# Residual sums in place, and four moves around the start of each attention layer

## The chip, the cores and the metric

The kernel runs on one core of one Trainium2 chip. The metric is device time in microseconds (us) of one execution, lower is better. The engines are named as in the profile: PE (matrix multiply; PEld is its weight load), DVE (vector), ACT (scalar, activations), POOL (GpSimd) and SP, whose queue issues nearly all DMAs. Each engine works through its own list of instructions in order and waits on semaphores for the others.

## The reference, cut to what matters

The input is one sequence of 2048 rows of 512 numbers. Four layers follow one another, spectral, attention, spectral, attention, and each adds its result to its input:

```python
x = x + A(layernorm(x)); x = x + B(layernorm(x)); x = x + A(layernorm(x)); x = x + B(layernorm(x))

A:  y = dft_seq_re @ (x @ dft_hid_re.T) - dft_seq_im @ (x @ dft_hid_im.T)

B:  q, k, v = x@wq, x@wk, x@wv            # 32 heads of 16, four segments of 512 rows
    for each segment s:
        a_dot = softmax(q_s k_s^T / 4 + causal mask) v_s
        a_mem = phi(q_s) M / (phi(q_s) z + 1e-6)         # phi(t) = t+1 if t>0 else exp(t)
        o_s   = sigmoid(beta) * a_mem + (1 - sigmoid(beta)) * a_dot
        M += phi(k_s)^T v_s;  z += sum of phi(k_s)
    return o @ wo
```

In the kernel the x that is added back is called the residual. In float32 each product is three matmuls over a high and a low part of both operands (`matmul3`, L106); `split` (L95) makes the two parts, the high one on ACT (L101) and the low one on DVE (L103).

## The kernel before, in words

The program is written as generators (a projection, a unit of softmax, a load with its split) that are placed into numbered slots by `place`; at the end the slots are run in order, and within a slot by a small order number. This gives the program order. PE keeps that order exactly. For the other engines and for the DMA queues a planner with a model of the times chooses the order, with the program order as priority; it may pull an instruction forward when the model shows its engine idle. Two kinds of instruction are pinned behind whatever stands just ahead of them on their engine in the program: the high part of a split on ACT, and the first statistics of a row, `bn_stats` (L139), on DVE. A tile with a tag shares a fixed number of buffers (`bufs`) with the others of that tag, and a new tile waits until a buffer is free.

A spectral layer ends with `hidden` for the first 1536 rows (products with the hidden DFT, 128 rows at a time into a PSUM tile `y`) and `hidden_last`, which works on four blocks of 128 rows at once, so that their four results come within a few matmuls of each other. Each result goes through `finish` (L164): DVE adds the residual rows `xr`, loaded with `load_rows` (L123), into a tile `xo`, and SP stores `xo` to DRAM (L167). `xo` has one buffer, so a sum waits until the store of the sum before has landed. All loaded rows (`xr`, the rows `xt` to be normalised, and raw weights `raw`) share the tag `xt` with four buffers of 2 KB per partition.

An attention layer has its own clock of slots; b is the slot at which its first unit starts. A unit is four heads of one segment; units follow every ten slots, eight in a segment of 80 slots, and two units make one head group g. For unit n at slot t = b + 10 n:

- `stack` loads its queries and keys (`stkq`, `stkk`) from DRAM, where the projection wrote them (`scrq`, `scrk`), at t - 21;
- `natural_max`, t - 17 to t - 7, makes the scores `nat` once to find each row's maximum: PE multiplies, DVE reduces (L605), then four small DVE operations (L621 to L628) write the maxima as three bf16 parts, `mparts`;
- `max_rows`, at t - 4, transposes `mparts` on PE into `mT`, ACT copies it to `mt` (L643), and a DMA on ACT's queue (L644) puts it into three extra rows of `stkq`;
- `softmax_values`, t to t + 12, makes the scores again, now with the maxima taken off (`sT`), the exponentials `pT`, and their product with the values (`pv_bank`).

What stands ahead of the first unit: `prep` normalises the rows of a segment, two blocks at a time: load, statistics, scaling to `xn` (L161), then PE transposes `xnT` and the split into `xT`. `proj` (PSUM tile `pqk`) makes queries and keys of one head group in 4 + 4 steps, `values` (`pvv`) makes the values in 16 steps. In the first segment head group 0 is projected from b - 34, the first eight steps of `values` stand at b - 26, head group 1 at b - 18, the second eight steps of `values` at b - 10. `hidden_last` of the spectral layer still runs from b - 26 to b - 12 beside them. The output weights `wo` are loaded and split by `load_split` at b - 14, b - 12, b - 10, b - 8, with the loads three slots sooner; the output projection that needs them first starts at b + 100. `prep` of the second segment has its transposes from b + 29 and b + 34 (t in the code), and its load, statistics and scaling 8, 5 and 3 slots ahead of that.

Of the kernel before, what the change touches and what calls it, by code (L numbers as in the profile page):

```python
# [10 lines left out]
F32 = mybir.dt.float32  # L11
# [3 lines left out]
ALU = mybir.AluOpType  # L15
# [3 lines left out]
P = 128  # L19
S, D, H = 2048, 512, 32  # L20
# [6 lines left out]
LT = L // P  # L27
# [34 lines left out]
def spectral_infini_kernel(  # L62
# [12 lines left out]
    nc = tc.nc  # L75
    V, A, G, T = nc.vector, nc.scalar, nc.gpsimd, nc.tensor

    consts = ctx.enter_context(tc.tile_pool(name="consts", bufs=1))
    sb = ctx.enter_context(tc.tile_pool(name="sb", bufs=1))
# [29 lines left out]
    def matmul3(ps, lhsT, rhs, first, last):  # L109
        T.matmul(ps, lhsT(0), rhs(0), start=first, stop=False)  # L110
        T.matmul(ps, lhsT(0), rhs(1), start=False, stop=False)
        T.matmul(ps, lhsT(1), rhs(0), start=False, stop=last)
# [4 lines left out]
    def bank(name, shape=(P, 512), dtype=F32):  # L117
        return psum.tile(list(shape), dtype, name=name, tag="bank", bufs=8)
# [2 lines left out]
        return sb.tile([P, 2, 512], dtype, name=name, tag=tag, bufs=bufs)  # L121

    def load_rows(src, name="xt"):  # L123
        t = sb.tile([P, 512], F32, name=name, tag="xt", bufs=4)
        nc.sync.dma_start(t, src)
        return t

# [7 lines left out]
    def row_stats(xts, mv):  # L135
        n = len(xts)
        for j, xt in enumerate(xts):
            st = sb.tile([P, 6], F32, name="st", bufs=2)
            pin(V.bn_stats(st, xt))  # L139
            V.bn_aggr(mv[:, j], st)  # L140
        ve = sb.tile([P, 2], F32, name="ve", bufs=3)[:, :n]
        V.tensor_scalar_add(ve, mv[:, :, 1], EPS)  # L142
        r = sb.tile([P, 2], F32, name="r", bufs=3)[:, :n]
        G.tensor_tensor(out=r, in0=ve, in1=half_neg[:, :n], op=ALU.pow)  # L144
        return ve, r

    def row_scale(rr, ve, r):
        t = sb.tile([P, 2], F32, name="rt", bufs=2)[:, : rr.shape[1]]
        V.tensor_tensor(out=t, in0=r, in1=r, op=ALU.mult)
        V.tensor_tensor(out=t, in0=t, in1=ve, op=ALU.mult)  # L150
        V.tensor_scalar(t, t, -0.5, 1.5, op0=ALU.mult, op1=ALU.add)
        V.tensor_mul(rr, r, t)
# [6 lines left out]
    def normal(xt, mv, rr):  # L159
        xn = sb.tile([P, D], F32, name="xn", bufs=2)  # L160
        V.tensor_scalar(xn, xt, mv[:, 0:1], rr, op0=ALU.subtract, op1=ALU.mult)  # L161
        return xn

    def finish(ps, xr, x_out, i, **where):  # L164
        xo = sb.tile([P, D], F32, name="xo", **(where or {"bufs": 1}))
        V.tensor_tensor(out=xo, in0=ps, in1=xr, op=ALU.add)  # L166
        nc.sync.dma_start(x_out[i], xo)  # L167
        return xo

    v_tiles = [consts.tile([P, H, VW], F32, name=f"vt{i}") for i in range(6)]  # L170
    v_count = [0]
# [7 lines left out]
    def place(order, gen, *at):  # L179
        for t in itertools.chain(*at):  # L180
            slots.setdefault(t, []).append((order, gen))

    def run_from(t, n, step=1):
        return range(t, t + n * step, step)
# [271 lines left out]
    def place_attention(x_in, x_out, t0, w_at, out_at):  # L456
# [3 lines left out]
        def prep(s, n):  # L460
            xt = [load_rows(x_in[s * LT + i]) for i in n]
            yield
            mv = sb.tile([P, 2, 2], F32, name="mv", bufs=2)
            ve, r = row_stats(xt, mv)
            yield
            rr = sb.tile([P, 2], F32, name="rr", bufs=2)
            row_scale(rr, ve, r)
            for j, i in enumerate(n):
                xn = normal(xt[j], mv[:, j], rr[:, j : j + 1])
                yield  # L470
                if i == 0:
                    xT[s] = sb.tile([P, 2, DT, 512], F32R, name="xT", bufs=1)
                pt = bank("xnT", (P, DT, P))
                for d in range(DT):
                    T.transpose(pt[:, d], xn[:, d * P : (d + 1) * P], ident)
                sl = slice(i * P, (i + 1) * P)
                split(xT[s][:, 0, :, sl], xT[s][:, 1, :, sl], pt)
                if j + 1 < len(n):
                    yield
            yield  # L480

        def values(s):
            vt[s] = {}
            for i in (0, 1, 3, 2):
                ps = bank("pvv")
                for d in range(DT):
                    matmul3(
                        ps,
                        lambda h: xT[s][:, h, d, i * P : (i + 1) * P],
                        lambda h: ws["v", d][:, h, :],  # L490
                        d == 0,
                        d == DT - 1,
                    )
                    if d + 1 < DT:
                        yield
                v = v_tiles[v_count[0] % len(v_tiles)]
                v_count[0] += 1
                A.activation(v[:, :, :DH], ps.rearrange("p (h d) -> p h d", d=DH), AF.Copy)
                vt[s][i] = v
                yield  # L500
# [390 lines left out]
        def outproj_split(s, i):  # L891
            n = (DT - 1) * P
            pt = bank("oT")
            for d in range(DT - 1):
                T.transpose(
                    pt[:, d * P : (d + 1) * P],
                    o_nat[s][i // 2][:, i % 2, d * P : (d + 1) * P],
                    ident,
                )
            t = pair("oh", "ut", 8)  # L900
            split(t[:, 0, :n], t[:, 1, :n], pt[:, :n])
            xr = load_rows(x_in[s * LT + i], "xr")
            yield
            ps = bank("po")
            for d in range(DT):
                src, c = (t, d) if d < DT - 1 else (oh[s, "last"], i)
                matmul3(
                    ps,
                    lambda h: src[:, h, c * P : (c + 1) * P],
                    lambda h: ws["o", d][:, h, :],  # L910
                    d == 0,
                    d == DT - 1,
                )
                yield
            finish(ps, xr, x_out, s * LT + i, tag="wd", bufs=8)
            yield

        def alloc_pv():
# [17 lines left out]
        def light(t, n=SU):  # L936
            return [k for k in range(t, t + n) if (k - t0) % SU not in (2, 4)]
# [5 lines left out]
        def post(t):  # L943
            return [t + 1, t + 2, t + 3]

        for k in range(4 * DT):
            n, d = "qkvo"[k // DT], k % DT
# [3 lines left out]
        for n in range(NSEG * USEG):  # L951
            t = t0 + SU * n
# [5 lines left out]
        for s in range(NSEG):  # L958
            b = t0 + SS * s
            for j in range(2):  # L960
                t = b - (43, 51, 60, 60)[s] + 5 * j
                place(2, prep(s, (2 * j, 2 * j + 1)), [t - 8, t - 5, t - 3, t, t, t + 2])
            place(2, values(s), *([light(b - 20), light(b)] if s else [run_from(b - 26, 8), light(b - 10)]))
            place(2, alloc_out(s), [b - 13])
            o = b + SS
            if s < NSEG - 1:
                free = light(o + 20) + light(o + 40) if s < NSEG - 2 else run_from(o + 20, DT * LT, 3)
            else:
                free = [out_at(k) for k in range(4 * LT)]
            if s == NSEG - 1 and x_out is out_tiles:  # L970
                for i in range(LT):
                    place(2, outproj_split(s, i), [o - 12 + i], range(o - 7 + 3 * i, o - 7 + 3 * i + 3), [o + 5 + 1, o + 7])
                place(1.5, transpose_last(s), [o + 5])
            else:
                for i in range(LT):
                    at = free[DT * i : DT * (i + 1)]
                    place(2, transpose_out(s, i), [at[0] - 4 - i % 2])
                    place(2, outproj(s, i), at)
            for g in range(NG):
                t = b + SG * g  # L980
                late = [] if s or g > 1 else [b + 3 + 2 * g]
                at = {
                    (0, 0): run_from(b - 34, 8),
                    (0, 1): run_from(b - 18, 8),
                    (0, 2): among(b, b + 13, 8),
                    (0, 3): among(b + 13, b + 29, 8),
                    (1, 0): among(b - 40, b - 29, 8),
                    (1, 1): among(b - 29, b - 17, 8),
                }.get((s, g), light(t - 50))
                place(2, proj(s, g, "q"), at[:4], post(at[3]))  # L990
                place(2, proj(s, g, "k"), at[4:], post(at[7]), late)
                if s > 0:
                    place(2, mem_read(s, g), [t - 12, t - 8])
                if s < NSEG - 1:
                    place(2, mem_update(s, g), [t + 6, t + 9] if g else [t + 16, t + 19])
# [11 lines left out]
    b2 = a2 + TC * 7 * HALF + LEAD  # L1007

    def w_at(b):
        return lambda k: b - 52 + 2 * k if k < 12 else b - 14 + 2 * (k - 12)  # L1010

    place_spectral(
        x_tiles, mids[0], a1, b1 - LEAD,
# [90 lines left out]
```

## Time and profile before

| | us |
|---|---|
| median of three runs (lowest, highest) | 1871.7 (1870.88, 1874.08) |
| profiled execution: time / span from first to last instruction | 1868.32 / 1866.6 |
| PE busy in the span | 1781.6 |
| first attention layer: first `mT` / first `pv_bank` of unit 0 | 479.66 / 497.55 |
| second attention layer: first `mT` | 1388.26 |

The times of the profile are microseconds from the first instruction. A row of the timeline gives start, duration, engine, line, operation, output tile <- input tiles, shapes, how many alike were merged, and in square brackets how long the engine had stood idle just before and what released it. PE's rows run into each other because a matmul's start overlaps the end of the one before. A row of the windows gives for a stretch A:B its length and the busy time and instruction count of PE, PEld, DVE, ACT and POOL, then the mean granted PE clock (1.00 is full speed), the DMA engines' busy share and GB/s. SPq and ACTq are the DMA issues of these engines.

### The profile page before, as it was taken

What the parts mean: (1) busy time and instruction counts of PE and PEld (TensorE: products, weight loads), DVE (VectorE), ACT (ScalarE), POOL (GpSimd) and SP (SyncE); (2) the same over time, 40 slices, a digit from 0 to 9 for tenths busy, and PEclk for the clock granted to TensorE, in tenths of its full rate; (3) what the DMA queues carried; (4) which work ended last, traced back from release to release, by engine and by line L of the source; (5) the groups of instructions that cost most, each with busy time, mean ns of one, the idle gap of its engine ahead of it and who ended that gap; (6) DMA issues with size and microseconds to landing.
All of it is one profiled execution on the core that took longest, in us unless ns stands there. A gap on an engine that the chain in (4) does not pass through costs nothing. (4 is left out here: it accounts for less than half of the span.)

```text
span 1866.6 us, 32022 instructions
## 1 busy us (share of the span) xinstructions
PE 1781.6 (95%) x10336; PEld 1291.0 (69%) x10336; DVE 1315.2 (70%) x4073; ACT 1056.1 (57%) x2292; POOL 526.1 (28%) x831
## 2 busy tenths in 40 slices
PE   7999999999889999999899999999988999999998
PEld 6788888888556666665468888778865566666555
DVE  7854544663787887877967686768557778787684
ACT  3222221432678787778864455444427877777785
POOL 4400000003345354445542000000124444444442
PEclk9999999999999999999999999999998999999999
DMA  6766556453534443435357687654544334344331
GB/s 214 225 217 214 189 181 210 161 170 127 177 125 134 131 134 104 147 119 181 106 170 231 196 259 215 180 170 141 172 144 142 121 113 150 120 132 136 121 122 51
DMA packets 165656, 296.50 MB, mean 159 GB/s; under 512 B 17776, under 2 KB 66928, under 8 KB 165488
## 3 DMA queue, kind: packets, MB, share of 16 engines
q1 hardware_dynamic: 162224, 293.68, 49.9%
q8 instruction: 81, 1.33, 0.3%
q10 hardware_dynamic: 3264, 0.79, 0.2%
q14 instruction: 87, 0.71, 0.1%
HBM read 192.95 MB, written 100.66 MB: 157 GB/s over the span
## 5 line engine op out<-in xcount | busy, mean ns | idle before, releaser
L605 DVE CUSTOM_DVE_ANT_0 junk<-nat,mask 128x512 bf16<-128x512 f32 (+3 forms) x1024 | 496.3, 485 | 196.6 <-PE nat L87 162.2
L671 ACT ACTIVATE pT<-sT 128x512 f32<-128x512 f32 x640 | 371.5, 599 | 13.5 <-ACT sT L670 1.7
L674 POOL TENSOR_SCALAR_AFFINE_SELECT pT<-pT 128x256 f32<-128x256 f32 (+1 forms) x448 | 198.6, 457 | 451.8 <-ACT pT L671 388.1
L87 PE MATMUL u<-chi,xa 128*128 128x512 f32 x1024 | 317.3, 391 | 7.3 <-DVE xa L99 7.3
L87 PE MATMUL sT<-stkq,stkk 99*128 99x256 bf16 (+3 forms) x1024 | 249.1, 306 | 10.1 <-DMA stkq<-mt 4.6
L87 PE MATMUL nat<-stkk,stkq 96*128 96x512 bf16 (+3 forms) x1024 | 247.0, 303 | 7.1 <-DVE mx L605 2.7
L670 ACT ACTIVATE sT<-sT 128x256 f32<-128x256 f32 (+1 forms) x640 | 207.3, 335 | 53.0 <-PE sT L87 48.3
L87 PEld LDWEIGHTS u<-chi,xa 128*128 128x128 f32 x1024 | 193.5, 189 | 47.2 <-ACT chi L101 7.3
L144 POOL TENSOR_TENSOR r<-ve,half_neg 128x2 f32<-128x2 f32 (+1 forms) x33 | 22.7, 688 | 665.2 <-DVE ve L142 660.1
L87 PE MATMUL u<-clo,xa 128*128 128x512 f32 x512 | 201.5, 394 | 2.4 <-DVE clo L103 2.0
L87 PE MATMUL y<-wdt,us 128*128 128x512 f32 x768 | 181.9, 390 | 0.0
L87 PEld LDWEIGHTS <-stkk 99*128 99x128 bf16 x1024 | 82.2, 99 | 136.7 <-issue 122.9
L87 PEld LDWEIGHTS y<-wdt,us 128*128 128x128 f32 x768 | 143.6, 188 | 29.7
L87 PE MATMUL pv_bank<-pT,vt 128*17 128x512 f32 (+3 forms) x2048 | 151.2, 435 | 0.0
L87 PEld LDWEIGHTS <-stkq 96*128 96x128 bf16 x1024 | 94.6, 99 | 62.4 <-issue 22.8
L87 PE MATMUL pvv<-wv,xT 128*128 128x512 f32 x384 | 129.8, 451 | 3.7 <-DVE mx L605 3.7
L87 PE MATMUL pqk<-xT,wq 128*128 128x512 f32 x384 | 130.3, 448 | 0.0
L87 PE MATMUL po<-wo,oh 128*128 128x512 f32 x384 | 122.3, 433 | 4.2 <-DVE mx L605 2.2
L87 PE MATMUL pqk<-xT,wk 128*128 128x512 f32 x384 | 124.7, 433 | 0.0
L87 PEld LDWEIGHTS u<-clo,xa 128*128 128x128 f32 x512 | 96.6, 189 | 26.6 <-DVE clo L103 6.7
L87 PEld LDWEIGHTS pv_bank<-pT,vt 128*17 128x17 f32 x2048 | 53.6, 97 | 85.9 <-issue 82.7
L101 ACT ACTIVATE chi<-cring 128x512 fp32r<-128x512 f32 x112 | 70.6, 630 | 69.3 <-DVE clo L103 35.0
(138 smaller groups left out, 3038.3 us busy)
## 6 DMA issues: line engine op xcount, KB each, us to landing
sum<-sring SPq DMA_DIRECT2D x32, 1024.0 KB
cring<-sum SPq DMA_DIRECT2D x128, 256.0 KB
stkq<-scrq SPq DMA_DIRECT2D x64, 384.0 KB
stkk<-scrk SPq DMA_DIRECT2D x64, 384.0 KB
cring<-in_ct SPq DMA_DIRECT2D x96, 256.0 KB
sring<-in_ct SPq DMA_DIRECT2D x32, 512.0 KB
xt<-mid SPq DMA_DIRECT2D x64, 256.0 KB
craw<-in_ct SPq DMA_DIRECT2D x30, 512.0 KB
```

What stands on the lines that cost most here:

```text
L87: return tc.keep_in_program_order(op(*args, **kwargs))
L101: pin(A.activation(hi, src, AF.Copy, scale=scale))
L144: G.tensor_tensor(out=r, in0=ve, in1=half_neg[:, :n], op=ALU.pow)
L605: V.tensor_tensor_reduce(junk[:, :n], src, mask[:, 512 - n :], 1.0, 3e38, ALU.add, ALU.min, dst,)
L670: A.activation(blocks, blocks, AF.Relu)
L671: A.activation(dst, ps, AF.Exp, scale=-SCALE)
L674: G.affine_select(blocks, blocks, pattern=[[0, n] for n in blocks.shape[1:-1]] + [[1, P]], compare_op=ALU.is_ge, fill=0.0, base=0, channel ...
```

## The change

It has five parts, in both attention layers alike, and the arithmetic is the same.

1. `finish` adds into the loaded residual tile itself and stores from there. The tile `xo` is gone, in the last output projection too, where it had the tag `wd`; the row tag `xt` gets a fifth buffer. The memory is the same. A row buffer is now held until its store has landed.
2. The output weights are loaded and split at b + 20, b + 25, b + 30, b + 35.
3. Head group 1 of the first segment is projected from b - 26.
4. The first eight steps of the first segment's `values` move to b - 18.
5. `prep` of the second segment has its load, statistics and scaling 18, 14 and 10 slots ahead of the transposes. The transposes stay.

```diff
     def load_rows(src, name="xt"):
-        t = sb.tile([P, 512], F32, name=name, tag="xt", bufs=4)
+        t = sb.tile([P, 512], F32, name=name, tag="xt", bufs=5)
...
-    def finish(ps, xr, x_out, i, **where):
-        xo = sb.tile([P, D], F32, name="xo", **(where or {"bufs": 1}))
-        V.tensor_tensor(out=xo, in0=ps, in1=xr, op=ALU.add)
-        nc.sync.dma_start(x_out[i], xo)
-        return xo
+    def finish(ps, xr, x_out, i):
+        V.tensor_tensor(out=xr, in0=ps, in1=xr, op=ALU.add)
+        nc.sync.dma_start(x_out[i], xr)
...
-            finish(ps, xr, x_out, s * LT + i, tag="wd", bufs=8)
+            finish(ps, xr, x_out, s * LT + i)
...
-                place(2, prep(s, (2 * j, 2 * j + 1)), [t - 8, t - 5, t - 3, t, t, t + 2])
-            place(2, values(s), *([light(b - 20), light(b)] if s else [run_from(b - 26, 8), light(b - 10)]))
+                first = (18, 14, 10) if s == 1 else (8, 5, 3)
+                place(2, prep(s, (2 * j, 2 * j + 1)), [*(t - d for d in first), t, t, t + 2])
+            place(2, values(s), *([light(b - 20), light(b)] if s else [run_from(b - 18, 8), light(b - 10)]))
...
-                    (0, 1): run_from(b - 18, 8),
+                    (0, 1): run_from(b - 26, 8),
...
-        return lambda k: b - 52 + 2 * k if k < 12 else b - 14 + 2 * (k - 12)
+        return lambda k: b - 52 + 2 * k if k < 12 else b + 20 + 5 * (k - 12)
```

## Prediction

> **What bounds the kernel now.** I read the page's busy times first, then PE's waits over the whole span, then the timeline of PE around the longest of them, and last what DVE and the DMA queue did there.
>
> ```profile
> PE 1781.6 (95%) x10336; PEld 1291.0 (69%) x10336; DVE 1315.2 (70%) x4073; ACT 1056.1 (57%) x2292; POOL 526.1 (28%) x831
> ...
> PE xnT L87 <- DVE xn L161: 18.2, 6, 4.8
> PE mT L87 <- DVE mparts L628: 13.1, 6, 5.5
> ...
> PE nat L87 <- DMA stkk<-scrk: 2.3, 1, 2.3
> ```
>
> PE sets the time: it is busy for 95% of the span, and its order is fixed. So only its idle time (85 us) and its clock can change much. The two largest waits are for the rows of a later segment (xnT) and for the first unit's maxima (mT). PE's timeline shows where they fall:
>
> ```profile
> 479.66 0.33 PE L87 MATMUL mT<-ident_b,mparts 128*80 128x128 bf16 x1 [4.97 <-DVE mparts L628]
> 479.75 1.63 PE L87 MATMUL pvv<-wv,xT 128*128 128x512 f32 x3
> 486.18 0.39 PE L87 MATMUL sT<-stkq,stkk 99*128 99x256 bf16 x2
> 486.44 1.04 PE L87 MATMUL pqk<-xT,wq 128*128 128x512 f32 x3
> 497.55 2.35 PE L87 MATMUL pv_bank<-pT,vt 128*17 128x512 f32 x32
> 511.14 2.35 PE L87 MATMUL pv_bank<-pT,vt 128*17 128x512 f32 x32
> 526.30 1.09 PE L87 MATMUL xnT<-ident,xn 128*128 128x128 f32 x4 [4.80 <-DVE xn L161]
> 529.88 2.52 PE L87 MATMUL pv_bank<-pT,vt 128*17 128x512 f32 x32
> ...
> 1388.26 0.33 PE L87 MATMUL mT<-ident_b,mparts 128*80 128x128 bf16 x1 [5.48 <-DVE mparts L628]
> 1394.47 0.39 PE L87 MATMUL sT<-stkq,stkk 99*128 99x256 bf16 x2
> 1411.30 0.58 PE L87 MATMUL nat<-stkk,stkq 96*128 96x512 bf16 x1 [2.30 <-DMA stkk<-scrk]
> 1437.32 1.09 PE L87 MATMUL xnT<-ident,xn 128*128 128x128 f32 x4 [4.79 <-DVE xn L161]
> ```
>
> The same two waits stand in both attention layers, and a third (nat, 2.30) in the second one only. After each the same matmuls are slow (three of pvv take 1.63, three of pqk later 1.04). The windows around them give the clock:
>
> ```profile
> 474.69:486.18 11.49, 6.52 (x20) 4.11 (x19) 8.96 (x35) 2.02 (x4) 0.79 (x1) 0.70 0.90 277
> 521.00:541.00 20.00, 13.94 (x99) 8.21 (x98) 18.86 (x68) 13.67 (x33) 7.14 (x13) 0.83 0.48 152
> 474.69:541.00 66.31, 54.07 (x356) 33.43 (x356) 54.27 (x217) 46.74 (x112) 25.89 (x43) 0.90 0.50 157
> 541.00:581.00 40.00, 39.23 (x288) 24.48 (x286) 31.02 (x125) 33.90 (x82) 21.01 (x32) 1.00 0.41 130
> 1382.78:1394.47 11.69, 6.21 (x19) 3.90 (x19) 9.81 (x36) 2.53 (x5) 1.22 (x1) 0.71 0.89 289
> 1410.00:1420.00 10.00, 8.70 (x44) 5.94 (x45) 5.70 (x27) 6.08 (x15) 3.25 (x7) 0.83 0.24 83
> 625.00:635.00 10.00, 7.84 (x69) 5.11 (x70) 9.79 (x31) 5.92 (x13) 6.17 (x9) 1.00 0.69 215
> ```
>
> A wait is paid twice: a mean of 0.70 over 11.49 us is 6.9 us at half speed. The row to remember for later is the second: DVE is busy 18.86 of 20 us.
>
> **Why the first maxima are late.** The DVE rows ahead of the first mT, and the DMA queue's:
>
> ```profile
> 471.76 0.69 DVE L166 TENSOR_TENSOR xo<-y,xr 128x512 f32<-128x512 f32 x1 [0.40 <-DMA mid<-xo]
> 475.20 0.08 DVE L605 DVE_READ_ACCUMULATOR2_ANT mx<- 128x1 f32 x1
> 476.56 0.69 DVE L166 TENSOR_TENSOR xo<-y,xr 128x512 f32<-128x512 f32 x1 [1.28 <-DMA mid<-xo]
> 477.16 0.17 DVE L621 SCALAR_TENSOR_TENSOR mparts<-mx 128x16 bf16<-128x16 f32 x1
> 477.86 0.69 DVE L103 TENSOR_TENSOR wo<-raw,wo 128x512 fp32r<-128x512 f32 x1
> 478.84 0.68 DVE L103 TENSOR_TENSOR wo<-raw,wo 128x512 fp32r<-128x512 f32 x1
> 479.44 0.17 DVE L628 SCALAR_TENSOR_TENSOR mparts<-mrem,mparts 128x16 bf16<-128x16 f32 x1
> ...
> 422.07 0.38 SPq L125 DMA_DIRECT2D raw<-in_wo  x1
> 468.07 0.35 SPq L125 DMA_DIRECT2D xr<-in_x  x1
> 468.47 0.42 SPq L167 DMA_DIRECT2D mid<-xo  x1
> 1390.65 0.32 SPq L576 DMA_DIRECT2D stkk<-scrk  x1
> ```
>
> Unit 0's last maximum is read at 475.20, and mparts is ready only at 479.6. In between DVE, in its own order, stood 1.28 for a store so that it could write the single xo, made that sum (0.60 to the next start), and put two splits of wo (0.60 from 478.84 to 479.44) between the four small operations. Before 475.20 it had lost 0.40 to another store, and two more wo splits and a phi of head group 1 there. A raw wo loaded at 422.07 also held one of four row buffers until its split, so that the last residual came only at 468.07.
>
> **The change part by part, against the profiled execution** (1868.32 us, span 1866.6; the median of the runs is 3.4 above it, and I carry the gain over to the median).
>
> A. Sums in place, wo away from here, head group 1 ahead of the values. The swap itself moves as many matmuls one way as the other, both from tiles that are ready, and the values are first used by pv_bank at 497.55; I cost it at nothing, covered by these 30 us; if that cover went, PE would wait for one ACT copy, some 0.6. DVE's remaining work up to the maxima (four sums, and reductions that follow PE) fits ahead of the moment at which PE reaches mT (479.66 - 4.97 = 474.69). So that wait goes. What is late next is the way from mT over ACT and the DMA into stkq, which the undisturbed end of this layer shows:
>
> ```profile
> 929.29 0.25 PE L87 MATMUL mT<-ident_b,mparts 128*80 128x128 bf16 x1 [1.14 <-DVE mparts L628]
> 933.90 0.59 PE L87 MATMUL sT<-stkq,stkk 99*128 99x256 bf16 x2 [3.71 <-DMA stkq<-mt]
> ```
>
> It takes 933.90 - 929.29 = 4.6. PE's work between mT and sT is 6.52 at about half speed, some 3.5 at full. The stage then lasts 4.6, of which 1.1 is a new wait at sT, instead of 11.49 and 11.69: 6.9 + 7.1 = 14.0 gained. Bounds: with the maxima still 2 late in each layer 10; with no new wait 16.
>
> B. Head group 1 written eight slots sooner. In the second layer unit 2's keys are loaded at 1390.65, because their projection ends late, and PE waits 2.30. Eight slots of about 1.36 us (ten take 511.14 - 497.55 = 13.6) are 11 us: the wait goes. The clock row 1410 to 1420 (0.83) is 3.4 us at half speed, about 2.9 of it after the wait: 1.45. Together 3.75; the first layer has no such wait. [...]
>
> C. Rows of the second segment ten slots sooner. The loads were early anyway; the statistics and scaling were not:
>
> ```profile
> 477.64 0.43 SPq L125 DMA_DIRECT2D xt<-mid  x1
> ...
> 518.24 0.68 DVE L139 BATCH_NORM_STATS2 st<-xt 128x6 f32<-128x512 f32 x1
> 525.61 1.00 DVE L161 TENSOR_SCALAR xn<-xt,mv,rr 128x512 f32<-128x512 f32 x2
> ...
> 630.12 0.63 PE L87 MATMUL xnT<-ident,xn 128*128 128x128 f32 x4 [2.16 <-DVE xn L161]
> ```
>
> Scaling moves by seven slots, 9.5 us; xn ended at 526.6 and would end near 517, while PE arrives at 526.30 - 4.80 = 521.5. The wait goes, 4.80 and 4.79; the clock row 521 to 541 (0.83) is 6.8 us at half speed, some 3.8 of it after the wait until pv_bank is normal again at about 530: 1.9 in each layer. Together 13.4. The waits of 2.16 in later segments stay.
>
> D. DVE pays. From 474.69 to 541 it is busy 54.27 of 66.31. Two sums and two wo splits move ahead of this stretch or out of it (4 x 0.60), leaving 51.9; the four wo splits come back at b + 20 to b + 35, 54.3 in all. After A and C the stretch would be 66.31 - 6.9 - 6.7 = 52.7. DVE's best share there is 18.86 of 20, 94%; at that it needs 55.2 without the splits and 57.8 with them, 2.5 or 5.1 too much. The planner can let splits slip into 541 to 581, where DVE has 9 us free; I take the middle, 3.8 in each layer, 7.6 lost. Bounds: 0, and all of C (6.7 in each layer). ACT gets the four high parts too, about 0.6 each, and is busy 46.74 of the 66: it follows.
>
> E. The fifth row buffer and the longer hold. A store issued at 468.47 released the sum at 471.76: 3.3 us longer for each buffer. Four residuals of hidden_last need four buffers and the fifth takes a row of segment two; residual loads stand far ahead of their sums (all but the one that wo held up). I take 0; a loss bound is one exposed store in each of the four layers, 13, and a gain 2. SP's queue gets fewer blocked issues before the first unit, and four loads more among the stacks, 256 KB each, beside DMA engines that are busy half the time.
>
> Sum: 14.0 + 3.75 + 13.4 - 7.6 = 23.6. 1868.3 becomes 1844.7, and the median 1871.7 becomes 1848.
>
> **The rivals.**
>
> *DVE takes back most of C.* For it: the share of 94% without the splits. One set of maxima in each layer then comes late by a few us, as at 929.29, and the next sT waits 3.71 and runs slow for about 1.9: 2 x 5.6 = 11 less gain, 1859. Against it: reductions have priority, and DVE has free time from 486 to 521.
>
> *Slower.* The same shortage, but lasting: wo splits and statistics stand in front of the maxima of units 2 to 5 in both layers. A late set costs what A is worth, about 7 to 8. It decides from the fourth of the eight units on (4 x 7 = 28 against 23.6); with all eight, 1848 + 56 = 1904, with five 1883. Against it: even in 521 to 541 the mT there waited little, and the splits can be done any time until b + 100.
>
> *The change doesn't do what it says.* DVE's order is the planner's: it may still put the sums between the last reduction and mparts. Then A saves only the stands for a store and the wo splits, 0.40 + 1.28 + 1.2 in each layer with the clock still dropping: about 6 instead of 14, 1856.
>
> *More gain.* DVE's shortage costs nothing (D is 0) and the new wait at sT doesn't show: 1848 - 7.6 - 2.2 = 1838.
>
> **How the numbers follow.** Forecast (1842 to 1855) 0.54; most of C taken back 0.20; planner keeps the sums 0.08; more gain 0.08; slower 0.10. The 8 in 10 range reaches from the gain case to somewhat above the first rival, 1838 to 1864. The measurement tells about 0.2%, 3.7 us, from no change. All cases but the slower one are faster; 0.03 from their edge may end within 0.2%: faster 0.87, same 0.03, slower 0.10.
>
> **What the profile after would show.** A: mT of unit 0 with an idle time below 1 in both layers, no wait for a store ahead of L166, the clock at 1.00 there, and a wait of about 1 at the first sT for stkq<-mt. B: no nat wait for stkk. C: bn_stats right after the pv_bank of unit 0, xnT of the second segment without a wait. D: wo splits among the maxima of units 2 to 4, DVE above 90% there, and small waits of PE on L605 or mparts. E: no PE wait for y or po on xr. The prediction is wrong if the time lost at unit 0 turns up whole in units 2 to 5, or if PE waits at the spectral layers' rows.

## The result, and the profile after

| | before | after |
|---|---|---|
| median (lowest to highest), five runs each on one chip, us | 1870.88 (1868.13 to 1874.08) | 1852.11 (1848.91 to 1853.03) |
| ratio after / before, 95% interval | | 0.9896 (0.9883 to 0.991) |
| profiled execution: time / span, us | 1868.32 / 1866.6 | 1848.91 / 1847.2 |

The kernel is 1.0% faster: 18.8 us by the medians, 19.4 by the profiled executions. The forecast was 1848 (1838 to 1864). The total hides that two of the five steps, A and B, came out for another reason than the one given; the experiments below show it.

The page of the kernel after, busy times, and PE's waits over the whole span (us in total, times, longest):

```profile
PE 1775.4 (96%) x10336; PEld 1284.1 (70%) x10336; DVE 1315.7 (71%) x4073; ACT 1054.6 (57%) x2292; POOL 526.3 (28%) x831
...
PE xnT L87 <- DVE xn L161: 9.8, 5, 2.2
...
PE mT L87 <- DVE mparts L626: 6.8, 9, 1.4
PE sT L87 <- DMA stkq<-mt: 6.5, 5, 3.8
```

The work is the same (10336 matmuls, DVE 0.5 us apart). The waits for rows fell from 18.2 to 9.8 and those for maxima from 13.1 to 6.8; the waits for `stkq<-mt` grew from 4.6 to 6.5. PE's busy time fell by 6.2, and the mean granted clock of the profiled execution rose from 0.989 to 0.997. PE's timeline after, at the places shown of before:

```profile
475.05 0.25 PE L87 MATMUL mT<-ident_b,mparts 128*80 128x128 bf16 x1 [0.53 <-DVE mparts L626]
478.71 0.40 PE L87 MATMUL sT<-stkq,stkk 99*128 99x256 bf16 x2
490.30 2.35 PE L87 MATMUL pv_bank<-pT,vt 128*17 128x512 f32 x32
504.13 2.35 PE L87 MATMUL pv_bank<-pT,vt 128*17 128x512 f32 x32
515.92 0.60 PE L87 MATMUL xnT<-ident,xn 128*128 128x128 f32 x4
518.09 2.35 PE L87 MATMUL pv_bank<-pT,vt 128*17 128x512 f32 x32
526.51 0.25 PE L87 MATMUL mT<-ident_b,mparts 128*80 128x128 bf16 x1 [1.42 <-DVE mparts L626]
532.12 2.35 PE L87 MATMUL pv_bank<-pT,vt 128*17 128x512 f32 x32
...
620.28 1.09 PE L87 MATMUL xnT<-ident,xn 128*128 128x128 f32 x4 [2.14 <-DVE xn L161]
921.05 0.25 PE L87 MATMUL mT<-ident_b,mparts 128*80 128x128 bf16 x1 [1.13 <-DVE mparts L626]
925.71 0.58 PE L87 MATMUL sT<-stkq,stkk 99*128 99x256 bf16 x2 [3.77 <-DMA stkq<-mt]
1296.27 0.66 PE L87 MATMUL xnT<-ident,xn 128*128 128x128 f32 x4 [1.20 <-DVE xn L161]
1376.51 0.25 PE L87 MATMUL mT<-ident_b,mparts 128*80 128x128 bf16 x1 [0.52 <-DVE mparts L626]
1521.98 0.63 PE L87 MATMUL xnT<-ident,xn 128*128 128x128 f32 x4 [2.16 <-DVE xn L161]
```

DVE's timeline has the four sums in one piece, with no wait for a store:

```profile
467.18 2.73 DVE L165 TENSOR_TENSOR xr<-y,xr 128x512 f32<-128x512 f32 x4 [0.57 <-PE y L87]
```

The 4.97 and 5.48 at the first mT are 0.53 and 0.52; the 4.80 at the second segment's rows is gone (515.92 has no bracket), and so is the nat wait of 2.30. New are the 1.42 at 526.51 (and the same at 1428.21) and the 1.20 at 1296.27. The windows give the clock:

```profile
474.52:478.71 4.19, 3.67 (x19) 2.33 (x19) 3.73 (x18) 0.67 (x2) 0.00 (x0) 1.00 0.27 67
518.09:532.12 14.03, 11.02 (x85) 5.79 (x84) 13.21 (x49) 12.48 (x31) 4.15 (x8) 1.00 0.66 209
610.00:630.00 20.00, 17.34 (x119) 11.71 (x117) 18.73 (x62) 14.35 (x35) 10.37 (x16) 0.91 0.48 150
1515.00:1535.00 20.00, 16.84 (x124) 11.52 (x123) 19.54 (x69) 14.69 (x35) 9.39 (x16) 1.00 0.54 172
915.00:935.00 20.00, 15.11 (x108) 8.88 (x101) 15.50 (x49) 14.63 (x34) 11.22 (x17) 0.83 0.41 132
```

The stage from the first mT to the first sT is the first row: 4.19 us at 1.00, where before it was 11.49 at 0.70. Half clock is what the windows show inside a slow stretch: 0.50 from 480 to 482 before, 0.50 from 621 to 623 after. The second row is where DVE is full now: 13.21 of 14.03 busy, and PE stands for 3.0 of it.

Where the 19.4 us came from can be read unit by unit, from the start of each unit's `pv_bank` before and after (497.55 - 490.30 = 7.25 for unit 0, and so on). Each row after the first is what that one unit adds to the gain; units that add or lose less than 0.8 are left out, but for unit 1. Unit 32 is the first of the second attention layer.

| unit | gained, us |
|---|---|
| unit 0 | 7.25 |
| unit 1 | -0.24 |
| unit 2 | 4.78 |
| unit 3 | -1.94 |
| unit 9 (the clock after the wait at 620.28) | -1.59 |
| unit 32 | 5.98 |
| unit 33 | 2.24 |
| unit 34 | 4.77 |
| unit 35 | -1.78 |

### The profile page after: what moved, and what is told of

It is laid out like the page before. It is cut to its first block, busy times and chain, and to the rows that moved or that the text cites. A ratio compares the mean times of both kernels' runs of the same rounds, so it can differ in the third digit from the quotient of the medians.

```text
span 1847.2 us, 31988 instructions
## 1 busy us (share of the span) xinstructions
PE 1775.4 (96%) x10336; PEld 1284.1 (70%) x10336; DVE 1315.7 (71%) x4073; ACT 1054.6 (57%) x2292; POOL 526.3 (28%) x831
```

## The experiments

The first five kernels each undo or shift one part of the change; the other six do one part alone, extend it, or test what was left. A ratio is against the kernel before on the same chip, with its 95% interval. "Lost" and "gained" at a unit are read like the table above, against the kernel after unless another is named. A stand is time in which an engine has an instruction next in its order but must wait for its input or its buffer.

**The separate sum tile put back** (four row buffers as before, the rest as after).

```diff
-        t = sb.tile([P, 512], F32, name=name, tag="xt", bufs=5)
+        t = sb.tile([P, 512], F32, name=name, tag="xt", bufs=4)
...
-    def finish(ps, xr, x_out, i):
-        V.tensor_tensor(out=xr, in0=ps, in1=xr, op=ALU.add)
-        nc.sync.dma_start(x_out[i], xr)
+    def finish(ps, xr, x_out, i, **where):
+        xo = sb.tile([P, D], F32, name="xo", **(where or {"bufs": 1}))
+        V.tensor_tensor(out=xo, in0=ps, in1=xr, op=ALU.add)
+        nc.sync.dma_start(x_out[i], xo)
+        return xo
...
-            finish(ps, xr, x_out, s * LT + i)
+            finish(ps, xr, x_out, s * LT + i, tag="wd", bufs=8)
```

> The changed kernel with the separate sum tile xo (one buffer) and four row buffers again; the other four parts stay. Theory: the store that each sum waits for is a part of A of its own. Four sums 3.3 us apart end some 10 us after the first, past the moment at which PE reaches the first mT, so a wait of 2 to 4 and half speed come back there: 6 to 14 us of the 19.4 are lost, ratio to before 0.993 to 0.997. Rival: the wo splits alone made the maxima late; then the first mT waits under 1 us and the ratio is that of the changed kernel, 0.988 to 0.991.

Measured: 1849.41, ratio 0.9893 (0.9867 to 0.9918), the same as the kernel after, as the rival has it. Its timeline of PE at the first mT:

```profile
476.20 0.25 PE L87 MATMUL mT<-ident_b,mparts 128*80 128x128 bf16 x1 [1.20 <-DVE mparts L628]
```

Its timeline of DVE at the same place:

```profile
470.75 0.69 DVE L166 TENSOR_TENSOR xo<-y,xr 128x512 f32<-128x512 f32 x1
...
473.77 0.69 DVE L166 TENSOR_TENSOR xo<-y,xr 128x512 f32<-128x512 f32 x1
...
476.57 0.69 DVE L166 TENSOR_TENSOR xo<-y,xr 128x512 f32<-128x512 f32 x1
```

The sums are still 3 us apart; with one `xo`, each has to follow the store of the one before. But none of these three has an idle time ahead of it: reductions fill the gaps. mT waits 1.20 instead of 0.53, and unit 0 starts 1.78 later. In the first layer 1.61 of that comes back at unit 9: the kernel after has its clock drop there, at 620.28, and its slowest `xnT` takes 0.45, while no `xnT` of this execution takes over 0.33. In the second layer unit 32 is level: the first mT waits 1.01 instead of 0.52, but the wait at 1296 isn't there. The stands for a store were not what made the maxima late.

**The output weights put back to their slots.**

```diff
-        return lambda k: b - 52 + 2 * k if k < 12 else b + 20 + 5 * (k - 12)
+        return lambda k: b - 52 + 2 * k if k < 12 else b - 14 + 2 * (k - 12)
```

> The changed kernel with the output weights at b - 14 to b - 8 again. Theory: two to four splits of 0.6 us and the row buffer held by a raw weight are the other part of A: the first mT waits 2 to 4 us in each layer, partly with half speed, 6 to 14 us lost, but units 2 to 4 get 2 x 2.4 us of DVE time back, so 2 to 10 lost in all, ratio 0.991 to 0.995. Rival: the stores alone made the maxima late; then the first mT waits under 1 us, and D is smaller: ratio 0.987 to 0.989, better than the changed kernel.

Measured: 1858.45, ratio 0.9941 (0.9923 to 0.9959). Its timeline of PE at the first mT:

```profile
478.80 0.33 PE L87 MATMUL mT<-ident_b,mparts 128*80 128x128 bf16 x1 [4.26 <-DVE mparts L626]
```

Its timeline of DVE ahead of that, the rows of the weights:

```profile
468.49 0.68 DVE L103 TENSOR_TENSOR wo<-raw,wo 128x512 fp32r<-128x512 f32 x1
...
472.97 0.69 DVE L103 TENSOR_TENSOR wo<-raw,wo 128x512 fp32r<-128x512 f32 x1 [0.96 <-ACT wo L101]
...
475.35 0.69 DVE L103 TENSOR_TENSOR wo<-raw,wo 128x512 fp32r<-128x512 f32 x1 [0.88 <-ACT wo L101]
...
477.59 0.69 DVE L103 TENSOR_TENSOR wo<-raw,wo 128x512 fp32r<-128x512 f32 x1
```

And its timeline of ACT, where two high parts wait for the load:

```profile
472.31 0.63 ACT L101 ACTIVATE wo<-raw 128x512 fp32r<-128x512 f32 x1 [1.53 <-DMA raw<-in_wo]
...
474.69 0.63 ACT L101 ACTIVATE wo<-raw 128x512 fp32r<-128x512 f32 x1 [1.75 <-DMA raw<-in_wo]
```

This is the old wait, with every other part of the change in place: 4.26 here and 4.52 in the second layer. Four splits of 0.60 are 2.4, and the two stands are 0.96 + 0.88, together 4.2; the mT starts 3.75 later than in the kernel after (478.80 against 475.05), so DVE could make up a little. The stands are a chain of two queues kept in order: DVE's low part waits for ACT's high part, which waits for a weight still on its way. Unit 0 loses 4.93 and unit 32 5.03, while units 3 and 35 gain 1.6 each. A wait of 2.00 for `stkk<-scrk` comes too, in the first layer (at 500.3), although head group 1 stands in its new, early slots: the weights also make the keys late.

**The swap undone** (head group 1 behind the first eight steps of the values again).

```diff
-            place(2, values(s), *([light(b - 20), light(b)] if s else [run_from(b - 18, 8), light(b - 10)]))
+            place(2, values(s), *([light(b - 20), light(b)] if s else [run_from(b - 26, 8), light(b - 10)]))
...
-                    (0, 1): run_from(b - 26, 8),
+                    (0, 1): run_from(b - 18, 8),
```

> The changed kernel with head group 1 projected behind the first eight steps of the values again. Theory: the keys of unit 2 come 11 us later, while PE is there about 7 us sooner than in the kernel before; so the wait for stkk is some 7 us more than before, that is 5 to 9 us in both layers, with half speed: 10 to 20 lost, ratio 0.994 to 1.000. Rival: the loads follow the earlier stage and the wait is that of before, 2.3 in the second layer only: ratio 0.990 to 0.992.

Measured: 1854.58, ratio 0.9915 (0.9886 to 0.9944), not separable from the kernel after. Unit 0 loses 1.47 and unit 32 2.05; units 1 and 33 give 0.3 and 0.6 of it back. In the second layer PE's timeline has its largest new wait for ACT, not for the keys:

```profile
1385.24 0.38 PE L87 MATMUL nat<-stkk,stkq 96*128 96x512 bf16 x1 [1.61 <-ACT pT L669]
```

The theory was far too large, and the rival met the ratio but not the wait that it gave for it. With the weights out of the way, the keys of head group 1 come nearly in time even from their old slots; the only wait for `stkk<-scrk` around these units is 0.78, in the first layer. So by this trace the swap is worth 1.2 and 1.5 us in the two layers, and the 2.30 of before was due to the weights for the larger part. By which way the weights held up the keys (ACT's order, DVE's or the DMA queue) was not tested.

**The rows of segment two put back** to 8, 5 and 3 slots ahead.

```diff
-                first = (18, 14, 10) if s == 1 else (8, 5, 3)
+                first = (8, 5, 3)
```

> The changed kernel with the second segment's rows at 8, 5 and 3 slots ahead again. Theory: the wait at xnT (4.8) and the half speed behind it come back in both layers and the small waits of units 2 and 3 go: the units' starts say that the rows' part gained 4.8 - 1.9 - 0.2 = 2.6 in the first layer, so 5 to 6 lost in both, ratio 0.992 to 0.993. Rival: with the other parts in place DVE reaches the rows in time by itself, or pays for them in full: ratio 0.989 to 0.990.

Measured: 1857.68, ratio 0.9934 (0.9912 to 0.9957). In its timeline of PE the old wait is back, and with it slow matmuls (3.71 for pv_bank, 2.35 in the kernel after with the clock at 1.00); the later mT waits little:

```profile
519.69 1.12 PE L87 MATMUL xnT<-ident,xn 128*128 128x128 f32 x4 [4.58 <-DVE xn L161]
...
523.29 3.71 PE L87 MATMUL pv_bank<-pT,vt 128*17 128x512 f32 x32
...
530.64 0.22 PE L87 MATMUL mT<-ident_b,mparts 128*80 128x128 bf16 x1 [0.20 <-DVE mx L603]
```

Unit 2 loses 4.90 and unit 3 gains 0.42; in the second layer 4.89 and 0.58. The part is worth 4.5 and 4.3, 8.8 in all by the profiled executions, more than the 5 to 6 expected.

**The output weights later still**, at b + 52 to b + 61.

```diff
-        return lambda k: b - 52 + 2 * k if k < 12 else b + 20 + 5 * (k - 12)
+        return lambda k: b - 52 + 2 * k if k < 12 else b + 52 + 3 * (k - 12)
```

> The changed kernel with the output weights loaded and split from b + 52 on, three slots apart, where DVE was busy for 78% only. Theory: the loss of 1.9 and 1.8 us that the units' starts show at unit 3 of each layer (mT waits 1.42, two nat waits of 0.7) is the price of the four wo splits on a DVE without free time. It goes: 3 to 4 us gained, ratio to before 0.987 to 0.988. Rival: the loss is the price of the rows' own work (statistics, scaling, splits of xT), which stays; ratio 0.989 to 0.990 and the mT wait of 1.4 stays.

Measured: 1847.6, ratio 0.9885 (0.9868 to 0.9901), which lies between the two expectations and overlaps the kernel after; the trace shows the place. Units 2 and 3 gain 1.08 and 1.62 in each layer, and in PE's timeline the 1.42 is halved:

```profile
524.15 0.25 PE L87 MATMUL mT<-ident_b,mparts 128*80 128x128 bf16 x1 [0.70 <-DVE mparts L626]
```

About half of the 2.7 is lost again at later units (1.3 at units 17 and 18, 1.2 at their match in the second layer). In the kernel after, DVE's timeline at this place reads:

```profile
520.84 0.68 DVE L103 TENSOR_TENSOR wo<-raw,wo 128x512 fp32r<-128x512 f32 x1
...
524.84 0.68 DVE L103 TENSOR_TENSOR xT<-xnT,xT 128x512 fp32r<-128x512 f32 x1
...
526.05 0.41 DVE L626 SCALAR_TENSOR_TENSOR mparts<-mrem,mparts 128x16 bf16<-128x16 f32 x1
...
526.86 0.68 DVE L103 TENSOR_TENSOR wo<-raw,wo 128x512 fp32r<-128x512 f32 x1
```

The splits of the rows (xT) and of the weights stand among the reductions and the four small operations of the maxima. The price of the weights' new place is that a full DVE (13.21 of 14.03 busy) has to make these splits too.

**The same ten slots for the rows of segments three and four.**

```diff
-                first = (18, 14, 10) if s == 1 else (8, 5, 3)
+                first = (18, 14, 10) if s else (8, 5, 3)
```

> The changed kernel with the rows of the third and fourth segment at 18, 14 and 10 slots ahead too. Theory: four waits of 2.15 us at xnT (units 9 and 17 of each layer) go, and with them the half speed that follows them in some runs: 8 to 12 us gained, ratio 0.984 to 0.986. Rival: DVE, 9.79 of 10 us busy around such a wait, gives the time back at the next maxima: ratio 0.988 to 0.990.

Measured: 1839.03, ratio 0.9834 (0.9819 to 0.9848), slightly better than the theory. All four waits of 2.15 are gone: units 9, 17, 41 and 49 gain 4.28 (with the clock), 2.97, 2.66 and 2.70. Some is lost at another place; PE's timeline there:

```profile
1291.64 0.66 PE L87 MATMUL xnT<-ident,xn 128*128 128x128 f32 x4 [2.39 <-DVE xn L161]
```

The window around it, from the windows of the same kernel:

```profile
1288.00:1298.00 10.00, 7.61 (x30) 5.80 (x29) 8.71 (x26) 4.27 (x11) 0.73 (x1) 0.83 0.61 199
```

The small wait at 1296 of the kernel after has grown to 2.39 and is followed by 3.4 us at half clock (0.17 x 10 x 2); unit 32 loses 3.52. Units 3 and 4 lose 2.4 more. There the clock is 0.83, where the kernel after has 1.00 from 518.09 to 545.84; the windows of this kernel show:

```profile
520.00:540.00 20.00, 17.02 (x125) 9.55 (x116) 15.83 (x64) 13.86 (x35) 4.49 (x11) 0.83 0.45 138
```

**The output weights alone**: the kernel before, with only their slots changed.

```diff
-        return lambda k: b - 52 + 2 * k if k < 12 else b - 14 + 2 * (k - 12)
+        return lambda k: b - 52 + 2 * k if k < 12 else b + 20 + 5 * (k - 12)
```

> The kernel before with the output weights at b + 20 to b + 35 and nothing else. Theory after the first runs: the splits, and the waits of ACT and DVE for their loads, made the maxima late (A, some 5 in each layer and the half speed) and held up the keys of unit 2 (B); with them gone alone the first mT waits 1 to 1.5 us and 10 to 14 us are gained, ratio 0.9925 to 0.995. Rival: the parts need each other; the sums' stores then stand where the splits stood, the first mT still waits over 3 us, ratio 0.997 to 1.000.

Measured: 1857.44, ratio 0.9941 (0.9924 to 0.9959): 11 us, over half of the whole change. Its timeline of PE, the first mT of each layer:

```profile
476.26 0.25 PE L87 MATMUL mT<-ident_b,mparts 128*80 128x128 bf16 x1 [1.51 <-DVE mparts L628]
...
1381.40 0.25 PE L87 MATMUL mT<-ident_b,mparts 128*80 128x128 bf16 x1 [1.39 <-DVE mparts L628]
```

With `xo` at one buffer and the projections in the old order, 4.97 and 5.48 become 1.51 and 1.39, and the nat wait of 2.30 is gone as well. Against the kernel before, units 0, 1, 32 and 33 gain 4.5, 1.2, 4.9 and 3.9; units 3 and 35 lose 1.9 and 0.9, with the rows where they were.

**The sums in place alone**: the kernel before, with only part 1 of the change (five row buffers, `finish` in the row tile).

```diff
-        t = sb.tile([P, 512], F32, name=name, tag="xt", bufs=4)
+        t = sb.tile([P, 512], F32, name=name, tag="xt", bufs=5)
...
-    def finish(ps, xr, x_out, i, **where):
-        xo = sb.tile([P, D], F32, name="xo", **(where or {"bufs": 1}))
-        V.tensor_tensor(out=xo, in0=ps, in1=xr, op=ALU.add)
-        nc.sync.dma_start(x_out[i], xo)
-        return xo
+    def finish(ps, xr, x_out, i):
+        V.tensor_tensor(out=xr, in0=ps, in1=xr, op=ALU.add)
+        nc.sync.dma_start(x_out[i], xr)
...
-            finish(ps, xr, x_out, s * LT + i, tag="wd", bufs=8)
+            finish(ps, xr, x_out, s * LT + i)
```

> The kernel before with the sums in place and five row buffers, and nothing else. Theory after the first runs: the planner already keeps the sums' stores apart, so the sums cost the path nothing, and the wo splits still make the maxima late; ratio 0.997 to 1.002, first mT wait over 3.5 us in both layers. Rival, the prediction's: the stands of 0.40 and 1.28 us for a store are on the path; the wait falls by about 2 in each layer, ratio 0.994 to 0.997.

Measured: 1870.83, ratio 0.9999 (0.9986 to 1.0011). The first mT still waits 4.71 and 4.59. In its timeline of DVE, the row that takes the place of the stand for a store:

```profile
475.40 0.69 DVE L103 TENSOR_TENSOR wo<-raw,wo 128x512 fp32r<-128x512 f32 x1 [1.45 <-ACT wo L101]
```

Before, DVE stood 0.40 + 1.28 for stores; without them it stands 1.45 for the next late thing, the weight. Alone, with the weights still there, the sums in place gain nothing that these runs can see (the interval is 0.14% to either side).

**Three edits together**: rows of all later segments sooner, weights at b + 52, separate sum tile with four row buffers.

```diff
-        t = sb.tile([P, 512], F32, name=name, tag="xt", bufs=5)
+        t = sb.tile([P, 512], F32, name=name, tag="xt", bufs=4)
...
-        V.tensor_tensor(out=xr, in0=ps, in1=xr, op=ALU.add)
-        nc.sync.dma_start(x_out[i], xr)
+        V.tensor_tensor(out=xo, in0=ps, in1=xr, op=ALU.add)
+        nc.sync.dma_start(x_out[i], xo)
...
-                first = (18, 14, 10) if s == 1 else (8, 5, 3)
+                first = (18, 14, 10) if s else (8, 5, 3)
...
-        return lambda k: b - 52 + 2 * k if k < 12 else b + 20 + 5 * (k - 12)
+        return lambda k: b - 52 + 2 * k if k < 12 else b + 52 + 3 * (k - 12)
```

> The changed kernel with the output weights from b + 52 on, the rows of all later segments sooner, and the separate sum tile with four row buffers again. Theory: the three gains add: 3.5 + 8 to 12 + 1 (the wait of 1.2 for the first rows of the second attention layer goes with the separate tile), ratio 0.982 to 0.984. Rival: DVE is the limit and the gains overlap: ratio 0.985 to 0.988.

Measured: 1831.97, ratio 0.9805 (0.979 to 0.9819), faster than both kernels and slightly better than the theory. Between the profiled executions it gains 16.9 on the kernel after, where the three edits alone gained 4.1, 9.3 and 0.6, together 14.0. The gains add up, and somewhat more, as neither the wait at 1296 nor the slow units 3 and 4 of the rows' run come here.

**The same with the sums in place** and five row buffers.

```diff
-        t = sb.tile([P, 512], F32, name=name, tag="xt", bufs=4)
+        t = sb.tile([P, 512], F32, name=name, tag="xt", bufs=5)
...
-        V.tensor_tensor(out=xo, in0=ps, in1=xr, op=ALU.add)
-        nc.sync.dma_start(x_out[i], xo)
+        V.tensor_tensor(out=xr, in0=ps, in1=xr, op=ALU.add)
+        nc.sync.dma_start(x_out[i], xr)
```

> The changed kernel with the output weights from b + 52 on and the rows of all later segments sooner; the sums stay in place with five row buffers. It differs from the run with the separate tile in that part alone. Theory: in place and separate are worth the same within 0.2%; in place gains some 1 us at the first unit of each layer and loses 1 to 2.5 us at the first rows of the second attention layer: ratio 0.979 to 0.983. Rival: with the other waits gone the sums in place show a gain of their own, ratio 0.976 to 0.978.

Measured: 1832.5, ratio 0.9791 (0.9775 to 0.9807), the same within the intervals. Unit 0 gains 1.16 against the kernel above, and unit 32 loses 3.6, with this row of PE's timeline ahead of it:

```profile
1287.38 0.66 PE L87 MATMUL xnT<-ident,xn 128*128 128x128 f32 x4 [2.55 <-DVE xn L161]
```

**The kernel after with four row buffers**, to see whether the longer hold of a buffer makes that wait.

```diff
-        t = sb.tile([P, 512], F32, name=name, tag="xt", bufs=5)
+        t = sb.tile([P, 512], F32, name=name, tag="xt", bufs=4)
```

> The changed kernel with four row buffers instead of five, sums in place. Theory: a buffer held until its store has landed makes the loads behind it late; with four, weights and rows of the spectral layers' last stage come later still, and the wait of 1.2 us for the first rows of the second attention layer grows to 2 to 6, and one shows in the first layer: ratio 0.990 to 0.994. Rival: that wait is the planner's order of DVE alone and doesn't depend on the buffers: it stays at 0.5 to 1.5, ratio 0.989 to 0.990.

Measured: 1853.9, ratio 0.9904 (0.9889 to 0.9918). Neither expectation held for the wait. Fewer buffers should have made the hold worse; instead the wait is gone. Its timeline of PE at the place:

```profile
1298.24 0.60 PE L87 MATMUL xnT<-ident,xn 128*128 128x128 f32 x4
```

Its timeline of DVE:

```profile
1296.76 1.00 DVE L161 TENSOR_SCALAR xn<-xt,mv,rr 128x512 f32<-128x512 f32 x2
...
1299.11 0.69 DVE L103 TENSOR_TENSOR wk<-raw,wk 128x512 fp32r<-128x512 f32 x1 [1.35 <-ACT wk L101]
```

Its timeline of SP's queue:

```profile
1295.61 0.33 SPq L125 DMA_DIRECT2D raw<-in_wk  x1
```

And the kernel after, first its timeline of DVE:

```profile
1293.25 0.69 DVE L103 TENSOR_TENSOR wk<-raw,wk 128x512 fp32r<-128x512 f32 x1 [1.81 <-ACT wk L101]
...
1295.67 1.00 DVE L161 TENSOR_SCALAR xn<-xt,mv,rr 128x512 f32<-128x512 f32 x2
```

Then its timeline of SP's queue:

```profile
1289.78 0.33 SPq L125 DMA_DIRECT2D raw<-in_wk  x1
```

In the kernel after, with the fifth buffer, the load of the first `wk` is issued 5.9 us ahead of the rows' scaling, and DVE's order has its split ahead of the scaling too. The weight is late, DVE stands 1.81 for it, and the scaling is queued behind. With four buffers the load goes out only 1.2 ahead, the split falls behind the scaling, and the stand of 1.35 keeps nobody. All eight kernels with five buffers have the split ahead of the scaling and this wait (0.28 to 2.55); all five with four, the kernel before among them, have it behind and no wait. The theory of the longer hold falls, and so does the rival: the wait is a matter of DVE's order, but the order depends on the buffers. Here other losses (1.4 at units 2 and 34, 2.3 and 1.5 at units 26 and 41) take back the gain. Why the planner orders it so in each case was not followed further.

## Why the prediction was right or wrong, step by step

The total was right: 23.6 us of gain forecast, 19.4 measured between the profiled executions (18.8 between the medians). The steps came out as follows.

| step | forecast, us | measured, us |
|---|---|---|
| A, first maxima, both layers | +14.0 | +14.8 (stages of 4.19 against 11.49 and 11.69) |
| B, head group 1 sooner, second layer | +3.75 | +2.2 (unit 33) |
| C and D, rows sooner, DVE pays | +5.8 | +5.8 (units 2 to 4: 2.79; 34 and 35: 2.99) |
| E, buffers and holds | 0 | -1.2 (wait at 1296) |
| not foreseen: clock drop at 620 | | -1.6 |

The sum is 20.0; the 0.6 that is left lies spread over other units.

**A: right in size, wrong in its cause.** The step named three things, the stands for a store (0.40 + 1.28), the sums, and the splits of wo, and gave the weights 0.60 each. The runs put it on the weights: moved alone they take 3.5 and 4.1 off the two waits, put back alone they bring waits of 4.26 and 4.52, and in place alone does nothing. What the step missed was the stand of DVE for a weight that had not landed. DVE's rows of before did not show it, because there the stand for a store covered it; ACT's did, and the step did not read them. From ACT's timeline of the kernel before:

```profile
475.94 0.63 ACT L101 ACTIVATE wo<-raw 128x512 fp32r<-128x512 f32 x1 [1.82 <-DMA raw<-in_wo]
```

This high part ends at 476.57, at the moment at which the store released DVE (476.56). The change takes the store, the sums and the weights away at once, so the gain did not depend on which of them was named; that the size came out right says nothing for the reading. The last 0.9 to 1 us of the wait is what sums in place and the swap take off together. The new wait of 1.1 at sT did not come: the way from mT to sT took at most 478.71 - 475.05 = 3.7, not the 4.6 read at 929.29 (still 925.71 - 921.05 = 4.7 in the kernel after), and PE's own work of 3.67 covers it.

**B: the mechanism was half the story.** The wait went, and the slow stretch behind it too: the clock is 1.00 from 1380 to 1412, as the step's 1.45 had it. But the swap was not needed for it: with the weights moved alone, and head group 1 in its old slots, the wait went as well, and unit 33 gains 3.9, as much as wait and slow stretch together. The step that failed is the one that put the late end of the projection down to its slots. The price was sized well. In the kernel after unit 33 gains 2.2, for the most part because new small waits of 0.5, 0.6 and 0.3 (for reductions and for ACT) stand in the same unit.

**C and D: the difference was right, each term too large.** C was put at 6.7 in each layer. With the weights later still, units 2 and 3 of each layer gain 5.5 and 5.7 against the kernel before: the waits of 4.8 are gone, but what was to come beside them, 1.9, is 0.7 and 0.9. D was put at 3.8; the weights at b + 20 cost the same units 2.7. Both terms were about 1.1 too large, and it is luck that the two errors cancel. (The rows put back gives 4.5 and 4.3: what C is worth while the weights' splits lie there.) The place of D, the maxima of units 2 to 4 with DVE at 13.21 of 14.03, was as forecast.

**E: a loss at a place that wasn't looked at.** The fifth buffer was costed as a hold (0, bounds +2 to -13). It did something else: with it a weight load goes sooner, and that weight's split stands ahead of the rows' scaling on DVE.

**The rivals.** DVE took back about half of C, 2.7 of 5.5, as step D had it, and not most of it. The maxima of later units were never late by more than 1.42, so the slower case did not begin. The planner did not keep a sum between the last reduction and mparts: the four sums end at 469.91, ahead of unit 0's last reductions. It did not do so with the sum tile put back either (there one sum, at 473.77, stands among the reductions), so no run shows what that would cost. Of the case of more gain one half came true, no wait at the first sT; the other half, D at nothing, did not.

## What to carry to other kernels

The row of a stand names only the last thing that the engine waited for. Take that away and the next late thing can stand in its place, as 1.45 for a weight did here when the 1.28 for a store was gone; before pricing a wait by its releaser, ask of each instruction queued there when its own input arrives. Work that nobody needs for 100 slots, such as a weight's split, is best kept out of the stretch that a chain of small operations must pass, and moving it alone was worth more than any other part of this change (11 us). An extra buffer is not only room: it can let a load, and the work behind it, go ahead of something more urgent (here a load 5.9 us ahead of the rows' scaling instead of 1.2).

## What the runs showed of the hardware

Short waits go with a drop of the clock at some places and not at others. In the kernel after, the wait of 2.14 at 620.28 is followed by slow matmuls (0.50 from 621 to 623, 0.91 over 20 us, 3.6 at half clock), the one of 2.16 at 1521.98 is not (1.00), and before, the 2.16 at 630.12 wasn't either (1.00 from 625 to 635). Four traces have 16 waits of 2.14 to 2.17: those of the kernels before and after, of the sums in place alone and of the kernel after with four row buffers. Slow matmuls follow 3 of them, the one at 620.28, one at 629.25 with the sums in place alone and one at 1525.66 with four row buffers. They follow all four waits of 2.30 to 2.55 that were read (2.30 before, 2.33 with the sums in place alone, 2.39 with the rows of all later segments sooner, 2.55 with the three edits and the sums in place). The 3.77 at 925.71 has a longer stretch (0.83 over 20 us, 6.8). The length of one wait does not settle it: with four row buffers a wait of 1.74 at 877.08 is followed by slow matmuls (0.63 for `nat`, 0.38 in the kernel after at 875.62), and 13 of the 16 above are not. The mean clock of the kernel after differs between its executions too: 0.997 in the profiled one (1848.91) and in that of 1850.63, 0.994 to 0.995 in those of 1852.11 to 1853.03.

Still open: the wait of 3.77 for `stkq<-mt` at 925.71 and its slow stretch stand in the fastest kernel too (4.85 there), and why this path takes 4.7 at the end of the layer and at most 3.7 at its start was not tried.
